# A convolution in float32 or in half-precision halves: the banded product of the later batches, its scales taken beforehand

## The chip, the core and the metric

The kernel runs on one core of a Trainium2 chip. The metric is the device time of one execution in microseconds (us). The core's engines run side by side, each through its own queue of instructions in order: PE (TensorE, matrix products, with its weight loads shown as PEld), DVE (VectorE), ACT (ScalarE), POOL (GpSimd) and SP (SyncE, which here only issues transfers). They wait for each other by semaphores. Transfers between the chip's memory and the on-chip memory are made by 16 DMA engines.

## The reference

Eight batches of 4224 tokens with 192 channels go through a causal convolution of 7 taps (one set of softmaxed taps for each of 8 groups of 24 channels), a two-dimensional Fourier transform of which the real part is added, a layer norm, and a two-layer network with a residual:

```python
w = softmax(weight)                                  # (8 heads, 7 taps)
x_pad = concat([zeros(B, 6, D), x], axis=1)
conv[b, s, h, g] = sum_k w[h, k] * x_pad[b, s + k, h, g]   # 8 heads of 24 channels
mixed = real(fft(fft(conv, axis=1), axis=2))
u = conv + mixed
un = (u - mean(u)) / sqrt(var(u) + 1e-6)
out = u + relu(un @ w_ch1) @ w_ch2                   # 192 -> 768 -> 192
```

## The kernel before

**The front of a batch.** A batch's tokens are cut into 36 windows of 128 rows that overlap, each giving 120 convolved tokens. Six windows make a chunk; a batch has 6 chunks. `load_windows` (L412) brings a chunk of 128 x 1152 float32 numbers into a tile `xt`, of which there are two. `squares` (L425) takes the sum of its squares on ACT; its written result, `sq`, is thrown away, only the running sum is kept. `conv_unit` multiplies the chunk with a banded matrix `band` (128 x 120, one for each head) in float32 on PE (L472), three heads into one piece of the fast accumulating memory, called `pc`; ACT moves `pc` into `xa` (L477), and SP stores `xa` to the scratch `sc` in memory. In the last batch PE takes only 7 heads; the eighth is done on DVE with multiply-adds (`conv_segments`, L542 and L544).

From all six sums `scales` makes a power of two, `s_x`, by which the batch is multiplied before it is cut into two half-precision numbers: the high half (ACT) and the rest (DVE). This is how every other product of the kernel runs: `a*b` as `a_hi*b_hi + a_hi*b_lo + a_lo*b_hi`. `load_x` reads the convolved tokens back in another order into `xs`, `split_x` makes `XH` (ACT, L633) and `XL` (DVE, L637) of them, and three stages of products, `pa` (L659), `pb` (L685) and `pq` (L755), do the Fourier transform.

**The back of a batch.** The transform's result, a residual, and a layer norm give `u`; its halves are turned by a transposing transfer into `kt`. The hidden layer is `ph` (L892), cut into the halves `hh` by ACT (L896) and `hlo` by DVE (L897); the output layer is `po` (L911, L914, L917). There are two buffers for `ph`, so the third `ph` waits until DVE has written the first one's `hlo`.

**The order.** After an opening, the program is a loop over 72 steps, 9 to a batch: 8 with 512 tokens of the network and one short one, the ninth, with 128. In step n of the loop the network of one tile is done, and around its products stand units of the fronts of later batches. `plan` says in which step, counted back from a batch's first network step, which unit stands: for the fourth batch and later the chunks of the convolution at -21 to -16, the scales at -15, the loads of `xs` from -14 and the splits of `xs` from -13. The scheduler that builds the program then sets the order in each engine's queue, down to single products. `in_turn()` puts a unit behind the latest `hh` and `hlo`, and `load_windows` puts its load behind the latest transposing transfer.

## Time and profile before

| what | value |
|---|---|
| runs (3) | 1234.21, 1235.25, 1237.3 us; median 1235.25 |
| profiled execution | 1241.18 us, span 1239.4 us |
| PE busy | 1172.8 us, 95% of the span |
| DVE busy | 807.2 us, 65% |
| ACT busy | 818.6 us, 66% |
| POOL busy | 501.1 us, 40% |
| granted PE clock, mean | 0.985 |
| moved | 170.14 MB, mean 137 GB/s |

The span runs from the first to the last instruction of the profiled execution. "Busy" is the time in which at least one instruction of the engine was under way. Products on PE overlap, so the mean duration of one is longer than the distance between the starts of two. In the rows below, "L472 PE MATMUL pc<-xt,band" reads: line 472, engine PE, operation, written tile, read tiles. A float32 product shows as two passes on PE.

### The profile page before, as it was taken

How to read it: one execution, taken by the hardware profiler on the slowest of the kernel's cores; microseconds unless marked ns; L12 is line 12 of the kernel's file. 1: busy time of each engine (PE TensorE's matmuls, PEld its weight loads, DVE VectorE, ACT ScalarE, POOL GpSimd, SP SyncE). 2: the span in 40 equal slices, each digit the busy share in tenths (PEclk: the TensorE clock that was granted, in tenths of full speed). 3: DMA queues.
4: the chain of work that ended last, by engine and by line, in shares of the span. 5: the costliest groups of instructions: out<-in, count | busy, mean ns of one | idle time of the engine just before them, and what ended most of it. 6: DMA issues, size and time to landing. Idle time of an engine off the chain costs nothing.

```text
span 1239.4 us, 30189 instructions
## 1 busy us (share of the span) xinstructions
PE 1172.8 (95%) x12234; PEld 933.0 (75%) x12234; DVE 807.2 (65%) x1998; ACT 818.6 (66%) x1581; POOL 501.1 (40%) x503
## 2 busy tenths in 40 slices
PE   5278899999999999999999999999999999999999
PEld 4276578787878878787877878788787867777777
DVE  4787575567666666667566676666865786556654
ACT  5476686678657876678656886578665676556542
POOL 2428233355244444445333552444443452346210
PEclk9599999999999999999999999999999999999999
DMA  8856784695435853486535754358452442323321
GB/s 261 316 149 150 163 207 133 171 215 149 108 100 155 211 139 79 120 204 174 136 93 157 190 149 109 96 150 207 108 126 78 122 90 68 78 68 87 74 53 46
DMA packets 225732, 170.14 MB, mean 137 GB/s; under 512 B 119151, under 2 KB 206925, under 8 KB 225592
## 3 DMA queue, kind: packets, MB, share of 16 engines
q1 hardware_dynamic: 212646, 141.03, 45.1%
q0 software_dynamic: 11136, 25.34, 7.0%
q8 instruction: 95, 1.56, 0.5%
q10 hardware_dynamic: 1810, 1.84, 0.5%
q14 instruction: 45, 0.37, 0.1%
HBM read 84.50 MB, written 58.50 MB: 115 GB/s over the span
## 4 chain that ended last, share of the span: by engine, by line
PE 78%; DVE 9%; ACT 5%; DMA 4%; issue 2%; another core or an unknown queue 1%; SPq 1%; POOL 1%; ACTq 0%; DVEq 0%
PE ph L892 30%; PE po L911 9%; PE po L917 9%; PE po L914 9%; PE pa L659 7%; PE pq L755 5%; PE pc L472 5%; PE pb L685 5%; DMA sc<-xa 2%; ACT un L835 1%; DVE XL L637 1%; DVE hlo L897 1%; ACT XH L633 1%; ACT hh L896 1%
## 5 line engine op out<-in xcount | busy, mean ns | idle before, releaser
L892 PE MATMUL ph<-kt,W 128*128 128x512 f16 (+1 forms) x2160 | 494.2, 362 | 9.9 <-DVE hlo L897 7.2
L897 DVE SCALAR_TENSOR_TENSOR hlo<-ph,hh 128x512 f16<-128x512 f32 (+1 forms) x400 | 271.1, 679 | 251.0 <-ACT hh L896 220.2
L896 ACT ACTIVATE hh<-ph 128x512 f16<-128x512 f32 (+1 forms) x400 | 237.2, 594 | 290.3 <-PE ph L892 266.9
L911 PE MATMUL po<-W,hh 128*128 128x192 f16 x1584 | 388.2, 246 | 2.7 <-ACT hh L896 1.7
L914 PE MATMUL po<-W,hh 128*128 128x192 f16 x1584 | 388.1, 246 | 2.2 <-DVE W L394 2.2
L917 PE MATMUL po<-W,hlo 128*128 128x192 f16 x1584 | 388.0, 247 | 1.5 <-DVE hlo L897 1.4
L892 PEld LDWEIGHTS <-W 128*128 128x128 f16 x2160 | 193.5, 98 | 153.1 <-issue 12.6
L791 POOL TENSOR_TENSOR u<-u,xr 128x768 f32<-128x768 f32 (+1 forms) x70 | 119.1, 1702 | 319.6 <-ACT u L790 286.1
L723 POOL DMA_INDIRECT xr<-sc,rows_sb x175 | 193.2, 1104 | 50.5 <-issue 34.8
L849 POOL TENSOR_TENSOR hl<-un,hl 128x512 f16<-128x512 f32 (+1 forms) x144 | 126.1, 898 | 145.9 <-ACT hl L846 120.4
L911 PEld LDWEIGHTS <-hh 128*128 128x128 f16 x1584 | 155.2, 98 | 19.7 <-ACT hh L896 2.2
L917 PEld LDWEIGHTS <-hlo 128*128 128x128 f16 x1584 | 154.9, 98 | 17.8 <-issue 2.6
L914 PEld LDWEIGHTS <-hh 128*128 128x128 f16 x1584 | 155.1, 98 | 16.4 <-issue 0.7
L668 DVE SCALAR_TENSOR_TENSOR yl<-pa,yh 99x512 f16<-99x512 f32 x128 | 86.6, 686 | 66.9 <-ACT yh L667 48.4
L835 ACT ACTIVATE un<-u,nm,y 128x192 f32<-128x192 f32 x256 | 119.5, 544 | 8.0 <-DVE nm L822 5.3
L659 PE MATMUL pa<-c_sb,XH 128*128 128x128 f16 x1024 | 105.5, 222 | 16.7 <-ACT XH L605 16.1
L472 PE MATMUL pc<-xt,band 128*120 128x144 f32 x756 | 109.3, 289 | 4.8 <-DVE V L694 3.4
L472 PEld LDWEIGHTS pc<-xt,band 128*120 128x120 f32 x756 | 100.4, 184 | 13.4 <-DVE V L694 3.8
L659 PEld LDWEIGHTS <-XH 128*128 128x128 f16 x1024 | 84.9, 104 | 28.4 <-ACT XH L605 16.2
L923 DVE SCALAR_TENSOR_TENSOR u<-po,fo,u 128x384 f32<-128x384 f32 (+1 forms) x136 | 80.6, 593 | 37.8 <-PE po L917 29.2
L637 DVE SCALAR_TENSOR_TENSOR XL<-xs,s_x,XH 128x768 f16<-128x768 f32 (+1 forms) x56 | 100.4, 1796 | 6.0 <-ACT XH L633 6.0
L755 PE MATMUL pq<-c_sb,V 128*128 128x130 f16 (+1 forms) x1440 | 96.6, 215 | 2.5 <-issue 2.5
(145 smaller groups left out, 1498.0 us busy)
## 6 DMA issues: line engine op xcount, KB each, us to landing
out_dram<-u SPq DMA_DIRECT2D x64, 384.0 KB
xt<-in_xw_dram SPq DMA_DIRECT2D x36, 576.0 KB
sc<-xa SPq DMA_DIRECT2D x33, 540.0 KB
xs<-sc SPq DMA_DIRECT2D x84, 192.0 KB
xs<-sc SPq DMA_DIRECT2D x28, 216.0 KB
xr<-sc SPq DMA_DIRECT2D x56, 96.0 KB
xt<-in_xv_dram SPq DMA_DIRECT2D x6, 504.0 KB
sc<-xa SPq DMA_DIRECT2D x6, 472.5 KB
```

Of the source, the lines that this page charges most:

```text
L472: nc.tensor.matmul(pc[:WR, h - h0], band[:, h], xt[:, :, h * GRP : (h + 1) * GRP], start=True, stop=True,)
L659: nc.tensor.matmul(pa[:, i], x[:, at], F[:, l], start=(n == 0), stop=(n == 2))
L723: nc.gpsimd.indirect_dma_start(bt.xr[it][:, g], None, bt.sc[: S if b else 128 * LP], bass.IndirectOffsetOnAxis(ap=(rows_sb if b else lines ...
L755: nc.tensor.matmul(po, weights(v, ND * r + k3), rhs[:, 0] if it == Q0 else rhs, start=(r + n == 0), stop=(r == 1 and n == 2),)
L835: nc.scalar.activation(un[:, g], u[:, g], AF.Identity, bias=nm[:, g : g + 1], scale=y[:, g : g + 1],)
L849: nc.gpsimd.tensor_tensor(bl[:, :, o : o + n], un[:, :ng, f], hi[:, :, f], op=ALU.subtract)
L892: nc.tensor.matmul(ph[:, n], W1[:, w, ht * 128 : (ht + 1) * 128], kt[:, k], start=(i == 0), stop=(i == len(order) - 1),)
L896: anchor[0] = nc.scalar.activation(hh, ph, AF.Relu).ins
L897: anchor[1] = nc.vector.scalar_tensor_tensor(hlo, ph, 0.0, hh, op0=ALU.max, op1=ALU.subtract).ins
L911: nc.tensor.matmul(po[:, g % 2], hh[:, ht, tk], W2[:, ht, 0], start=(ht == 0), stop=False)
L914: nc.tensor.matmul(po[:, g % 2], hh[:, ht, tk], W2[:, ht, 1], start=False, stop=False)
L917: nc.tensor.matmul(po[:, g % 2], hlo[:, ht, tk], W2[:, ht, 0], start=False, stop=(ht == 5),)
```

## The change

For batches 5 to 8 of the eight (numbers 4 to 7 in the code):

- Each chunk is loaded twice. The first time only its squares are summed (`measure`); the square is written over the chunk itself. This stands at -26 to -23 (a step later for the first of these batches).
- `scales` moves from -15 to -23 (-22 for the first).
- The second time the chunk is multiplied by the scale and split into halves (`split_window`, ACT and DVE), in the step before its convolution; the halves lie in a fixed tile `CV`.
- `split_band`, once, turns `band` into halves, scaled by 2^14, in place.
- Each head's product is three half-precision products into the same `pc`; ACT multiplies by the inverse scale `cg` as it moves `pc`.
- Loads are no longer issued by the convolution but by whoever has finished with a chunk (`next_load`), in one row over all these batches.
- In the last batch `conv_segments` moves from -16 to -25, and its square comes after its multiply-adds.

The tile `CV` also takes over the places of three smaller ones (the thrown-away squares, the scratch of the weights' conversion, and `w2f`).

```diff
+NB1 = 4
+BSC = 2.0 ** 14
...
+    CV = cp.tile([128, 4, 3 * D], F32, name="CV")
+    sq = CV[:, 0].bitcast(mybir.dt.bfloat16)
...
+    def split_band():
+        f = band.rearrange("p h o -> p (h o)")
+        n = NH * WR
+        hi, lo = (CV[:, i].bitcast(F16)[:, :n] for i in range(2))
+        nc.scalar.activation(hi, f, AF.Copy, scale=BSC)
+        nc.vector.scalar_tensor_tensor(
+            lo, f, BSC, hi, op0=ALU.mult, op1=ALU.subtract
+        )
+        both = f.bitcast(F16)
+        nc.vector.tensor_copy(both[:, :n], hi)
+        nc.vector.tensor_copy(both[:, n:], lo)
...
+    def split_window(bt, ch, l):
+        hi, lo = window_halves(bt, ch)
+        xt = bt.xt[ch]
+        with in_turn():
+            if l == 0:
+                nc.scalar.activation(hi, xt, AF.Copy, scale=bt.c)
+            else:
+                nc.vector.scalar_tensor_tensor(
+                    lo, xt, bt.c, hi, op0=ALU.mult, op1=ALU.subtract
+                )
+                next_load()
...
-            if b > 1:
+            if 1 < b < NB1:
                 squares(bt, xt)
...
+        if b < NB1:
+            terms, scale = ((band, xt),), 1.0
+        else:
+            halves = band.rearrange("p h o -> p (h o)").bitcast(F16).rearrange(
+                "p (l h o) -> p l h o", l=2, h=NH
+            )
+            hi, lo = window_halves(bt, ch)
+            terms, scale = ((halves[:, 0], hi), (halves[:, 0], lo), (halves[:, 1], hi)), bt.cg[:WR]
         for h in range(h0, h0 + n):
-            nc.tensor.matmul(
-                pc[:WR, h - h0], band[:, h], xt[:, :, h * GRP : (h + 1) * GRP],
-                start=True, stop=True,
-            )
-        to = xa[:, :, h0 * GRP : (h0 + n) * GRP].rearrange("p w (h g) -> p h w g", g=GRP)
-        nc.scalar.activation(to, pc[:WR, :n], AF.Copy)
+            for i, (w, x) in enumerate(terms):
+                nc.tensor.matmul(
+                    pc[:WR, h - h0], w[:, h], x[:, :, h * GRP : (h + 1) * GRP],
+                    start=(i == 0), stop=(i == len(terms) - 1),
+                )
+        nc.scalar.activation(to, pc[:WR, :n], AF.Copy, scale=scale)
...
+    def measure(bt, ch):
+        squares(bt, bt.xt[ch], bt.xt[ch])
+        next_load()
+
+    def front_later(bt, rel):
+        units = []
+        first = bt.b == NB1
+        sums_at = (
+            {-25: [0], -24: [1, 2], -23: [3, 4], -22: [5]}
+            if first
+            else {-26: [0], -25: [1, 2], -24: [3, 4], -23: [5]}
+        )
+        if bt.b >= NB0 and rel == -25:
+            units += [call(scratch, bt), call(conv_segments, bt)]
+        if first and rel == -23:
+            units.append(split_band)
+        units += [call(measure, bt, ch) for ch in sums_at.get(rel, ())]
+        if rel == plan(bt.b)[1]:
+            stages = scales(bt)
+            units += [call(next, stages), call(next, stages), call(last, stages)]
+        conv = [call(conv_unit, bt, rel + 21, p) for p in range(3) if -21 <= rel < -15]
+        units += conv
+        if -22 <= rel < -16:
+            if not conv:
+                units += [int] * 4
+            units += [call(split_window, bt, rel + 22, l) for l in range(2)]
+        return units
```

The change moves instructions in three places that matter below.

DVE, in the sixth step of each batch's nine (the rows are those of the fourth batch's): `hlo_5` are the six halves of that step, one for each `ph_5`; `XL` is a split of `xs` for a later batch. Before:

```order
L897 SCALAR_TENSOR_TENSOR hlo_5_9490<-ph_5_1_9532,hh_5_9489 128x512
L694 SCALAR_TENSOR_TENSOR V_0_9540<-pb_0_1_9559,V_0_9540 128x102x4
L923 SCALAR_TENSOR_TENSOR u_4_8480<-po_4_0_9506,fo,u_4_8480 128x384
L897 SCALAR_TENSOR_TENSOR hlo_5_9490<-ph_5_2_9636,hh_5_9489 128x512
L897 SCALAR_TENSOR_TENSOR hlo_5_9490<-ph_5_3_9670,hh_5_9489 128x512
L798 BN_STATS st_8_9682<-u_8_9577 128x6
L637 SCALAR_TENSOR_TENSOR XL<-xs_0_9455,s_x_9195,XH 128x64x12
L923 SCALAR_TENSOR_TENSOR u_4_8480<-po_4_2_9650,fo,u_4_8480 128x384
L799 BN_AGGR mv_8_9683<-st_8_9682 128x2
L897 SCALAR_TENSOR_TENSOR hlo_5_9490<-ph_5_4_9708,hh_5_9489 128x512
L897 SCALAR_TENSOR_TENSOR hlo_5_9490<-ph_5_5_9718,hh_5_9489 128x512
```

With the change:

```order
L939 SCALAR_TENSOR_TENSOR hlo_5_9731<-ph_5_1_9810,hh_5_9730 128x512
L679 SCALAR_TENSOR_TENSOR XL<-xs_0_9649,s_x_7292,XH 128x64x12
L965 SCALAR_TENSOR_TENSOR u_4_8671<-po_4_0_9747,fo,u_4_8671 128x384
L939 SCALAR_TENSOR_TENSOR hlo_5_9731<-ph_5_2_9879,hh_5_9730 128x512
L939 SCALAR_TENSOR_TENSOR hlo_5_9731<-ph_5_3_9912,hh_5_9730 128x512
L840 BN_STATS st_8_9924<-u_8_9819 128x6
L965 SCALAR_TENSOR_TENSOR u_4_8671<-po_4_2_9892,fo,u_4_8671 128x384
L841 BN_AGGR mv_8_9925<-st_8_9924 128x2
L939 SCALAR_TENSOR_TENSOR hlo_5_9731<-ph_5_4_9949,hh_5_9730 128x512
L939 SCALAR_TENSOR_TENSOR hlo_5_9731<-ph_5_5_9960,hh_5_9730 128x512
L474 SCALAR_TENSOR_TENSOR CV<-xt_0_9423,s_x_9722,CV 128x1152
L736 SCALAR_TENSOR_TENSOR V_1_10007<-pb_1_0_10008,V_1_10007 128x102x4
```

The split `XL` went from behind the fourth `hlo_5` to behind the second, and the new split of a chunk, `CV`, stands behind the sixth.

DVE, where the last batch's multiply-adds `sg` stand. Before they begin in the second step of the sixth batch, behind both `XL` of that step:

```order
L897 SCALAR_TENSOR_TENSOR hlo_1_13020<-ph_1_3_13182,hh_1_13019 128x512
L637 SCALAR_TENSOR_TENSOR XL<-xs_3_12651,s_x_11509,XH 128x64x12
L798 BN_STATS st_4_13195<-u_4_13104 128x6 x2
L923 SCALAR_TENSOR_TENSOR u_0_12158<-po_0_2_13162,fo,u_0_12158 128x384
L542 TENSOR_SCALAR sg_13461<-xg_13459,taps 128x792
L799 BN_AGGR mv_4_13196<-st_4_13195 128x2 x2
L897 SCALAR_TENSOR_TENSOR hlo_1_13020<-ph_1_4_13230,hh_1_13019 128x512
```

With the change they begin nine steps earlier, in the second step of the fifth batch, and share it with a chunk's split:

```order
L679 SCALAR_TENSOR_TENSOR XL<-xs_3_10611,s_x_7292,XH 128x64x12
L579 TENSOR_SCALAR sg_11545<-xg_11543,taps 128x792
L581 SCALAR_TENSOR_TENSOR sg_11545<-xg_11543,taps,sg_11545 128x792
L939 SCALAR_TENSOR_TENSOR hlo_1_11016<-ph_1_3_11191,hh_1_11015 128x512
L840 BN_STATS st_4_11214<-u_4_11101 128x6 x2
L581 SCALAR_TENSOR_TENSOR sg_11545<-xg_11543,taps,sg_11545 128x792
L965 SCALAR_TENSOR_TENSOR u_0_10087<-po_0_2_11159,fo,u_0_10087 128x384
L841 BN_AGGR mv_4_11215<-st_4_11214 128x2 x2
L581 SCALAR_TENSOR_TENSOR sg_11545<-xg_11543,taps,sg_11545 128x792
L939 SCALAR_TENSOR_TENSOR hlo_1_11016<-ph_1_4_11251,hh_1_11015 128x512
L474 SCALAR_TENSOR_TENSOR CV<-xt_5_10778,s_x_9722,CV 128x1152
```

Two of the seven now stand between the third and the fourth `hlo_1`, where there was only `XL`, and the chunk's split follows the fifth.

SP, between two transposing transfers `kt` of the fourth batch; `xt` are loads of chunks, `xr` and `out_dram` the network's own. Before:

```order
L859 DMA_TRANSPOSE kt_5_9173<-hl_5_9104 128x12x128
L931 DMA out_dram<-u_2_8049 128x768
L714 DMA xr_1_9801<-sc_5299 128x1x192
L859 DMA_TRANSPOSE kt_6_9468<-hl_6_9410 128x12x128
L931 DMA out_dram<-u_3_8294 128x768
L412 DMA xt_0_9487<-in_xw_dram 128x1152
```

With the change:

```order
L901 DMA_TRANSPOSE kt_5_9405<-hl_5_9351 128x12x128
L973 DMA out_dram<-u_2_8208 128x768
L411 DMA xt_5_9408<-in_xw_dram 128x1152
L411 DMA xt_0_9423<-in_xw_dram 128x1152
L756 DMA xr_1_10044<-sc_5302 128x1x192
L411 DMA xt_1_9690<-in_xw_dram 128x1152
L973 DMA out_dram<-u_3_8468 128x768
L901 DMA_TRANSPOSE kt_6_9704<-hl_6_9654 128x12x128
```

Three loads stand between the two transposing transfers where there was none; each waits for ACT to have squared the chunk that lay in its tile.

More of the change, by code (lines that the diff above doesn't have):

```diff
@@ L338, in square_w @@
             mlp["n" + name] = sb.tile([128, 2], F32, tag="nrm2", name=f"nrm_{name}")
-        sq = sb.tile(
-            [128, 1152], mybir.dt.bfloat16, tag="sq", name=f"sq_{name}_{col}", bufs=1
-        )
         nc.scalar.activation(
@@ L354, in convert @@
         else:
-            bits, aux = (
-                sb.tile([128, 3 * D], F32, tag=f"cv{i}", name=f"cv{i}_{name}", bufs=1)
-                for i in range(2)
-            )
+            bits, aux = CV[:, 1], CV[:, 2]
             if name[-1] == "0":
-                dst = cp.tile([128, 3 * D], F32, name="w2f")
+                dst = CV[:, 3]
             else:
@@ L413, in load_windows, with squares @@
         bt.xt[ch] = xt
-    def squares(bt, x):
+    def squares(bt, x, to=None):
         if bt.nsq == 0:
@@ L418, in squares @@
         n = x.shape[1] if len(x.shape) == 2 else x.shape[1] * x.shape[2]
-        sq = sb.tile(
-            [128, 1152], mybir.dt.bfloat16, tag="sq", name=f"sq_{bt.b}_{bt.nsq}", bufs=1
-        )[:, :n]
-        if len(x.shape) == 3:
-            sq = sq.rearrange("p (w d) -> p w d", w=x.shape[1])
+        if to is None:
+            to = sq[:, :n]
+            if len(x.shape) == 3:
+                to = to.rearrange("p (w d) -> p w d", w=x.shape[1])
         with in_turn():
             nc.scalar.activation(
-                sq, x, AF.Square, accum_out=bt.nrm[:, bt.nsq : bt.nsq + 1]
+                to, x, AF.Square, accum_out=bt.nrm[:, bt.nsq : bt.nsq + 1]
             )
@@ L448, in scratch, with window_halves @@
         bt.sc = dp.tile([S + DUP, D], F32, tag="sc", name=f"sc_{bt.b}", bufs=4)
+    def split_band():
[9 more added lines that the diff above has]
+        nc.vector.tensor_copy(both[:, n:], lo)
+    def window_halves(bt, ch):
+        n = WC * bt.xt[ch].shape[2]
+        return tuple(
+            CV[:, 2 * (ch % 2) + l].bitcast(F16)[:, :n].rearrange("p (w d) -> p w d", w=WC)
+            for l in range(2)
+        )
[10 more added lines that the diff above has]
+                next_load()
     def conv_unit(bt, ch, part, xa_slot=("xa", 2)):
@@ L454, in conv_unit @@
         if part == 0:
-            if ch == 0:
+            if ch == 0 and b < NB0:
                 scratch(bt)
-            if b > 1:
+            if 1 < b < NB1:
                 squares(bt, xt)
@@ L534, in conv_segments @@
         acc = sb.tile([128, SR, DH], F32, tag="xs", name=f"sg_{bt.b}", bufs=2)
-        squares(bt, x.rearrange("p r d -> p (r d)"))
         for i in range(NH - HP):
@@ L546, in conv_segments @@
                     )
+        flat = x.rearrange("p r d -> p (r d)")
+        squares(bt, flat, flat)
         for base, n in ((0, 128), (S, 32)):
@@ L560, in scales @@
         nc.vector.reciprocal(bt.g, bt.c)
+        if bt.b >= NB1:
+            bt.cg = sb.tile([128, 1], F32, tag="cg", name=f"cg_{bt.b}")
+            nc.vector.tensor_scalar_mul(bt.cg, bt.g, 1.0 / BSC)
         nc.vector.tensor_scalar_mul(bt.g, bt.g, GSC)
@@ L981, in plan, with later_loads, next_load @@
         splits = {-13: [0], -12: [1], -11: [2, 3], -10: [4], -9: [5], -8: [6, 7]}
-        return {r: [r + 21] for r in range(-21, -15)}, -15, loads, splits, later_a
+        scales_at = -15 if b < NB1 else -22 if b == NB1 else -23
+        return {r: [r + 21] for r in range(-21, -15)}, scales_at, loads, splits, later_a
+    def later_loads():
+        for b in range(NB1, B):
+            for k in range(2 * NCH):
+                yield b, k % NCH
+    wanted = later_loads()
+    def next_load():
+        b, ch = next(wanted, (None, 0))
+        if b:
+            load_windows(batches[b], ch)
+    def measure(bt, ch):
[8 more added lines that the diff above has]
+            else {-26: [0], -25: [1, 2], -24: [3, 4], -23: [5]}
+        )
+        if bt.b >= NB0 and rel == -25:
[13 more added lines that the diff above has]
+        return units
     def front(bt, rel):
@@ L986, in front @@
         conv, scales_at, load_at, split_at, a_at = plan(bt.b)
-        if bt.b >= NB0 and rel == scales_at - 1:
-            units.append(call(conv_segments, bt))
+        if bt.b >= NB1:
+            units, conv, scales_at = front_later(bt, rel), {}, None
         for ch in conv.get(rel, ()):
@@ L992, in front @@
                 units.append(call(load_windows, bt, ch + 2))
+            if bt.b == NB1 - 1 and ch + 2 >= NCH:
+                units.append(next_load)
         if bt.b == 2 and rel == min(conv) - 1:
             units += [call(load_windows, bt, ch) for ch in range(2)]
-        if bt.b > 2 and rel in (min(conv) - 2, min(conv) - 1):
+        if bt.b > 2 and conv and rel in (min(conv) - 2, min(conv) - 1):
             units.append(call(load_windows, bt, rel - min(conv) + 2))
```

2 lines of the change are left out of this document (1 added, 1 removed).

## The prediction, as it was put on record before the run

> **What bounds the kernel now.** First the page: span, busy times, and the span in 40 slices.
>
> ```profile
> span 1239.4 us, 30189 instructions
> PE 1172.8 (95%) x12234; PEld 933.0 (75%) x12234; DVE 807.2 (65%) x1998; ACT 818.6 (66%) x1581; POOL 501.1 (40%) x503
> ...
> PE   5278899999999999999999999999999999999999
> ...
> PEclk9599999999999999999999999999999999999999
> ```
>
> After the opening, some 200 us, PE is busy in every slice, at nearly the full granted clock. "Busy" does not say that PE runs at its pace, since products overlap; so I go to single steps of the loop. The windows below (bounds: the first `ph` of a step, from the timeline) are the sixth step of the fourth batch, the ninth, and the first three of the fifth batch; the columns are the width, then busy time with counts of PE, PEld, DVE, ACT and POOL, then clock, DMA share and GB/s.
>
> ```profile
> 641.20:657.40 16.20, 15.57 (x178) 11.78 (x177) 9.17 (x20) 9.28 (x17) 6.61 (x7) 1.00 0.39 106
> 690.90:701.20 10.30, 10.30 (x144) 10.30 (x143) 5.93 (x16) 8.87 (x18) 3.75 (x5) 1.00 1.07 246
> 701.20:716.70 15.50, 15.50 (x171) 11.97 (x170) 10.21 (x24) 12.34 (x27) 8.87 (x10) 1.00 0.73 187
> 716.70:732.20 15.50, 15.50 (x141) 11.99 (x139) 12.09 (x31) 14.11 (x26) 9.36 (x9) 1.00 0.56 152
> 732.20:750.10 17.90, 17.90 (x184) 14.54 (x182) 11.36 (x32) 12.00 (x24) 6.50 (x7) 1.00 0.63 155
> ```
>
> PE fills its window in all but the first. Whether it also runs at its pace, the chain of waits tells (start, length, what): it runs for long stretches from product to product on PE itself.
>
> ```profile
> 644.67 1.16 PE pq L755 x35
> 677.89 1.02 PE pq L755 x18
> 699.42 1.98 PE pc L472 x16
> 703.96 2.19 PE pb L685 x48
> 706.15 2.16 PE ph L892 x10
> 843.59 1.74 PE pc L472 x14
> ```
>
> The half-precision products take 2190/48 = 45.6 ns for 102 columns, 1020/18 = 56.7 for 130 and 216 for 512: about 0.416 ns a column and 2.7 ns beside. So PE streams; what is taken from it there is taken from the time. Where it idles in this part, DVE is what it waits for, in two places only:
>
> ```profile
> 657.38 1.24 PE L892 MATMUL ph<-kt,W 128*128 128x512 f16 x5 [0.63 <-DVE hlo L897]
> 876.85 1.24 PE L892 MATMUL ph<-kt,W 128*128 128x512 f16 x5 [0.92 <-DVE hlo L897]
> 893.31 1.24 PE L892 MATMUL ph<-kt,W 128*128 128x512 f16 x5 [0.30 <-DVE hlo L897]
> 896.20 0.26 PE L911 MATMUL po<-W,hh 128*128 128x192 f16 x1 [0.63 <-ACT hh L896]
> ```
>
> **The product on PE.** These are the groups of instructions, the first from a window that holds the convolutions of the last four batches alone.
>
> ```profile
> L472 PE MATMUL pc<-xt,band 128*120 128x144 f32 x372 | 55.1, 288 | 0.0
> L472 PEld LDWEIGHTS pc<-xt,band 128*120 128x120 f32 x756 | 100.4, 184 | 13.4 <-DVE V L694 3.8 <-ACT xa L477 1.4 <-DVE band L234 1.0
> L755 PEld LDWEIGHTS <-V 128*64 128x64 f16 x288 | 9.6, 111 | 3.6 <-issue 3.2
> L892 PEld LDWEIGHTS <-W 128*128 128x128 f16 x2160 | 193.5, 98 | 153.1 <-issue 12.6 <-DMA kt<-hl 1.9
> ```
>
> 372 passes are 186 float32 products (18 chunks of 8 heads, 6 of 7). By the chain 16 passes take 1.98 us and 14 take 1.74: 248 ns for a head. Three half-precision products of 144 columns, between the 56.7 of 130 and the next wider, come to 2.7 + 144 x 0.416 = 62.6 ns each, 188 a head. That is 60 ns less, over 186 heads **-11.2 us**. It lies wholly on PE's path.
>
> This needs the weight loads to stay hidden: one of 120 columns every 62.6 ns, where float32 had one every 124. The trace has no half-precision load of 120 columns. Two rows bound it: float32 loads of 120 columns keep up with 124 ns, at twice the bytes; half-precision loads of 64 columns keep up with 1160/35 = 33 ns, which makes 62 ns for 120. Both ends come to 62, the products' own pace, so I take them as hidden, with a thin margin. The full duration of a load, 111 ns, would be the price if none ran ahead of its product (a rival, below).
>
> The 64-column loads take longer (111 ns) than the 128-column ones (98), so width 128 has a quicker way. The Trainium skill says why ("TensorE: Matmul & The Clock Gate", "Weight-path perf modes"): the fast weight load is on for exactly 128 columns that are not float32, so 120 columns would go without it; and the same page ("LDWEIGHTS") gives columns/1.2 ns, 100 ns for 120. By that figure a head would take 300 ns and the change lose 186 x 52 ns = 9.7 us. The trace disagrees with the figure: 64 columns would then need 53 ns, and they keep up with 33.
>
> **The splits.** Each of 24 chunks gets one more ACT instruction (to the high half) and one more DVE instruction (the rest). Nearest rows are the splits of the weights, contiguous as these are, and the square of the same width:
>
> ```profile
> L379 DVE SCALAR_TENSOR_TENSOR W<-w1a,s_w,W 128x768 f16<-128x768 f32 x1 | 1.0, 1018 | 0.0
> L394 DVE SCALAR_TENSOR_TENSOR W<-w2f,s_w,W 128x576 f16<-128x576 f32 x1 | 0.9, 869 | 0.0
> L371 ACT ACTIVATE W<-w1a,s_w 128x768 f16<-128x768 f32 x1 | 0.9, 922 | 0.0
> L425 ACT ACTIVATE sq<-xt 128x1152 bf16<-128x1152 f32 x42 | 49.1, 1169 | 3.6 <-DMA xt<-in_xw_dram 3.6
> L425 ACT ACTIVATION_READ_ACCUMULATOR sq<-xt 128x1 f32 x48 | 9.9, 206 | 0.0
> ```
>
> DVE: 1018 + 384 x (1018 - 869)/192 = 1316 ns, and 1.5 us if it grows with the width alone; I take 1.4, in all 34 us. ACT: 1.2 us, in all 29. Both are behind PE's work: they stand in the sixth to the ninth and the first two steps of each nine. The tightest is the second (716.70): DVE 12.09 + 1.4 of 15.0 us, ACT 14.11 + 1.2 of the same, so ACT is full. But the convolution's square leaves this step and another's comes last in it, and the third step has 6 us of room. If a DVE split delays PE by half of itself in each tight step (two a batch), the cost is 4 x 2 x 0.7 = 5.6 us; if it hides, 0. I take **+1.0**.
>
> The squares stay as many as they were (1169 + 206 ns); what they write becomes float32 in place, a form the trace lacks. At twice the write time it would add 1.2 us to ACT in steps that have 6 to 7 us free: 0 either way. Splitting `band` is five small instructions in one step, hidden too.
>
> **What moves on DVE.** At 657.38 PE waits for `hlo`, because this stands ahead of it (DVE's timeline, and the waits in total):
>
> ```profile
> 653.80 2.35 DVE L637 SCALAR_TENSOR_TENSOR XL<-xs,s_x,XH 128x768 f16<-128x768 f32 x1
> ```
>
> It recurs once in each of four batches. With the change `XL` stands two `hlo` earlier, where the next `ph` comes only after 36 `pq` products (1.16 us) and 18 `po` (192 columns, by the line above 82.6 ns each, 1.49 us) and finds DVE done. Gain 4 x 0.63 = 2.5 us if nothing takes its place, 0 if the chunk's split behind the sixth `hlo` does. I take **-1.5**.
>
> The last batch's multiply-adds are seven of these:
>
> ```profile
> L544 DVE SCALAR_TENSOR_TENSOR sg<-xg,taps,sg 128x792 f32<-128x792 f32 x6 | 6.2, 1030 | 0.0
> L542 DVE TENSOR_SCALAR sg<-xg,taps 128x792 f32<-128x792 f32 x1 | 1.4, 1440 | 0.0
> ```
>
> 7.6 us. Where they stood PE lost 0.92 + 0.30 + 0.63 = 1.85 us; that goes. Where they go, 716.70 to 750.10, DVE has 12.09 + 11.36 = 23.45 us, and with 7.6 and 1.4 comes to 32.5 of 33.4 - 0.9 = 32.5. PE's `ph` of that step come 2.3 to 3.3 us apart (chain of waits):
>
> ```profile
> 722.08 1.08 PE ph L892 x5
> 724.40 1.08 PE ph L892 x5
> 727.72 1.08 PE ph L892 x5
> ```
>
> From the third `hlo` on the order puts about 4 us of DVE work between two `hlo`; DVE falls about 6 us behind, and the two `ph` buffers cover some 5. I expect 1.2 us of waiting there, at best 0, at worst 5: net **-0.6** (-1.85 to +3).
>
> **Transfers.** 18 x 576 KB + 6 x 504 KB = 13.4 MB more, 3.5 in a stretch of nine steps that moves 144.7 us x 144 GB/s = 21 MB:
>
> ```profile
> 411.90:556.60 144.70, 144.07 (x1532) 115.73 (x1530) 94.33 (x236) 102.25 (x199) 62.67 (x61) 1.00 0.57 144
> ```
>
> The DMA share is 0.39 to 0.73 but for the short ninth step (1.07), where one chunk is loaded as before. A load is issued about a step ahead of its use, 10 to 17 us. On SP three loads now stand ahead of a transposing transfer, and each waits for a square on ACT; behind them wait `xr`, `out` and `kt`, and PE needs `kt` a step later. The squares they wait for stand in the step before, so I cost this at 0; a late load has cost 3 us at worst so far:
>
> ```profile
> POOL u L791 <- DMA xt<-in_xw_dram: 6.1, 2, 3.0
> ```
>
> **Sum.** -11.2 + 1.0 - 1.5 - 0.6 = -12.3 us on the profiled execution's span of 1239.4 us (1241.18 with what lies around it). The runs' median is 1235.25, 0.5% below; the difference is the same there: **1223.0 us**.
>
> **Rivals.**
>
> *The other engines fill up.* ACT at 15.3 of 15.0 us in the second step and DVE at 32.5 of 32.5 where `sg` goes hold `hh` and `hlo` back. For it: these sums. Against: PE lost nothing in that step with ACT at 14.11 of 15.5, and both neighbours have room. At the upper bounds, 5.6 for the splits and 3 for `sg`, with no gain from `XL`: -11.2 + 8.6 = -2.6; about half of that is likelier, -11.2 + 4.3 = -6.9: 1228.
>
> *The weight loads set the pace (slower than before).* Place: each of the 558 new products. If a load does not run ahead, a product takes the load's 111 ns instead of 62.6: 333 a head against 248, 186 x 85 ns = 15.8 us more, 1251. It decides from 83 ns a load on, where the gain is zero. For it: 120 is not 128, and the margin is thin. Against: the 33 ns of the 64-column loads. The skill's 100 ns is this same rival, at 1245.
>
> *The second loads come late.* Four batches with one 3 us wait each on PE eat 12 us: 1235, no change. For it: three loads in a row on SP. Against: they are issued a step ahead.
>
> *More is won*, all of DVE's waits gone and no new ones: -11.2 - 2.5 - 1.85 = -15.6, 1219.7.
>
> **Chances.** Forecast 0.66 (its own range 1219.5 to 1227), engines full 0.18, more 0.04, weight loads 0.06, late loads 0.06. Under 0.3% (3.7 us) a difference cannot be told from none. The first three are faster by more: 0.88, with nearly all of the second in it; same 0.06; slower 0.06. The range 1218.5 to 1232 leaves out the last two and the edges.
>
> **What would show it.** `pc` in the later batches: three products a head, 62 to 63 ns from start to start, 24 in 1.5 us; weight loads in between without gaps. If they are 80 or more apart, the loads set the pace. In the windows of a batch (9 steps) the width falls from 144.7 to about 141.3, by 2.9 for the product and some 0.5 for `XL`. At the sixth step the 0.63 us wait is gone. Where `sg` stands, one or two waits of PE for `hlo`, 1 to 2 us in all. Behind the fifty-first step nothing changes, and nothing ahead of the tenth. The forecast is wrong if PE shows idle time ahead of `pc` with ACT or DVE `CV` as releaser, or behind `kt`.

## The result, and the profile after

| | before | with the change |
|---|---|---|
| median of the runs | 1235.25 us (1231.83 to 1237.3, 15 runs) | 1226.54 us (1224.16 to 1233.09, 15 runs) |
| profiled execution | 1241.18 us, span 1239.4 us | 1226.07 us, span 1224.3 us |

The ratio is 0.9934, 95% interval 0.9921 to 0.9946: 8.7 us, 0.7% faster. Beside the experiments the changed kernel was timed twice more, on the chips called C and D below: 0.9934 (0.9912 to 0.9956) and 0.9967 (0.9953 to 0.9982).

The page of the changed kernel: span and busy times.

```profile
span 1224.3 us, 30643 instructions
PE 1161.2 (95%) x12420; PEld 919.4 (75%) x12420; DVE 848.3 (69%) x2029; ACT 850.9 (70%) x1606; POOL 502.2 (41%) x503
```

PE has lost 11.6 us of busy time, DVE gained 41 and ACT 32. PE's share of the span stays at 95%, and the span is shorter, so most of the new work on DVE and ACT (now 69 and 70%) lies beside PE's. The profiled spans are 15.1 us apart, but 5.6 us of that lie ahead of step 10 and 1.4 behind step 50, where both kernels issue the same instructions in the same order; that is the difference of two executions (a second profile of the kernel before reaches step 10 at 277.1 us, the changed kernel at 277.3). Steps are counted from 0, as in the code. So all that follows is read from the **stretch** from the first `ph` of step 10 to that of step 50, where the change is. Windows of the kernel before, then of the changed one (first the nine steps of the third batch, 18 to 26, that took 144.7 us before, then the whole stretch):

```profile
282.90:932.30 649.40, 644.66 (x6812) 515.85 (x6809) 432.75 (x1068) 455.99 (x884) 277.86 (x265) 1.00 0.56 140
```

```profile
405.50:548.30 142.80, 141.93 (x1577) 112.62 (x1577) 104.19 (x241) 110.07 (x204) 62.56 (x61) 1.00 0.68 169
277.30:918.60 641.30, 636.08 (x7000) 503.66 (x6997) 472.23 (x1099) 488.56 (x909) 278.16 (x265) 1.00 0.67 164
```

8.1 us less in the stretch, close to the 8.7 of the medians. A second profile of the kernel before gave 649.4 again.

The product itself, by the groups of instructions of the stretch, and a piece of PE's timeline (the float32 rows stand in the prediction):

```profile
L511 PE MATMUL pc<-CV,band 128*120 128x144 f16 x558 | 44.8, 226 | 0.0
L511 PEld LDWEIGHTS <-band 128*120 128x120 f16 x558 | 41.6, 133 | 5.4
```

```profile
657.02 0.73 PE L511 MATMUL pc<-CV,band 128*120 128x144 f16 x9
```

No idle time ahead of any of the 558. By the chain of waits nine of them follow one another in 0.56 us, 62.5 ns each. A weight load takes 133 ns from its start to its end and holds nothing up.

PE's waits in the stretch (in all, times, longest), before and after:

```profile
PE ph L892 <- DVE hlo L897: 4.1, 7, 0.9
PE po L911 <- ACT hh L896: 0.6, 1, 0.6
```

```profile
PE ph L934 <- DVE hlo L939: 3.2, 9, 0.6
PE ph L934 <- DMA kt<-hl: 1.1, 2, 0.7
PE po L953 <- ACT hh L938: 0.5, 2, 0.3
```

4.7 us in 8 waits became 4.8 us in 13. The waits did not go away, they moved. Each costs PE about 0.16 us more than the row says, since the idle time counts from the end of the last product, and that runs on behind the point at which the next could have started (five `ph` show as 1.24 us before a gap and take 1.08 in a stream).

To see where, I took from each step's length the time of its products at their own pace (columns x 0.4167 ns + 3 ns; 248 ns for a float32 head). What is left is the **loss** of the step. In us, for the kernel before and for three profiles of the changed one (the second and third from C and D):

| | before | changed | 2nd | 3rd |
|---|---|---|---|---|
| products at their pace | 642.3 | 631.3 | 631.3 | 631.3 |
| sixth steps (14, 23, 32, 41) | 3.8 | 1.3 | 1.3 | 1.3 |
| where `sg` stands (37, 38, 46, 47) | 2.8 | 2.2 | 2.3 | 2.8 |
| second steps (10, 19, 28) | 0.2 | 1.9 | 2.2 | 2.8 |
| eighth steps (16, 25, 34, 43) | -0.2 | 1.2 | 1.2 | 1.2 |
| ninth steps (17, 26, 35, 44) | -0.2 | 1.4 | 3.8 | 0.6 |
| fourth and fifth steps | 1.0 | 1.8 | 1.8 | 1.8 |
| first steps (18, 27, 36, 45) | 0.0 | 0.4 | 2.1 | 3.1 |
| third and seventh steps | -0.4 | -0.3 | -0.3 | -0.3 |
| stretch | 649.4 | 641.3 | 645.7 | 644.6 |

The product gives 11.0 us, the sixth steps 2.6, and on balance some 5.5 us of new losses come back. What those are, the rows show in four places.

*Second steps.* ACT's timeline of the changed kernel at the end of step 28 (start, length), and PE's:

```profile
575.37 0.58 ACT L938 ACTIVATE hh<-ph 128x512 f16<-128x512 f32 x1
575.84 1.25 ACT L472 ACTIVATE CV<-xt,s_x 128x1152 f16<-128x1152 f32 x1
576.99 0.83 ACT L888 ACTIVATE hl<-un 128x768 f16<-128x768 f32 x1
577.72 0.99 ACT L515 ACTIVATE xa<-pc,cg 120x432 f32<-120x432 f32 x2
578.61 1.08 ACT L938 ACTIVATE hh<-ph 128x512 f16<-128x512 f32 x2
...
579.25 0.26 PE L953 MATMUL po<-W,hh 128*128 128x192 f16 x1 [0.25 <-ACT hh L938]
579.98 0.59 PE L934 MATMUL ph<-kt,W 128*128 128x512 f16 x2 [0.33 <-DVE hlo L939]
```

The new split, `hl` and two evictions stand between two `hh`; `hh` comes late, `hlo` after it, and PE waits for both.

*Eighth steps.* DVE's timeline in step 34:

```profile
674.33 3.57 DVE L679 SCALAR_TENSOR_TENSOR XL<-xs,s_x,XH 128x768 f16<-128x768 f32 x2
677.82 0.67 DVE L939 SCALAR_TENSOR_TENSOR hlo<-ph,hh 128x512 f16<-128x512 f32 x1
```

Both `XL` of the step now stand between two `hlo`; before there was an `hlo` between them.

*Ninth steps.* SP's timeline in step 26, before and after (the time is that of issuing):

```profile
547.13 1.96 SPq L859 DMA_TRANSPOSE kt<-hl  x1
549.18 1.90 SPq L438 DMA_DIRECT2D sc<-xa  x2
```

```profile
535.15 1.81 SPq L630 DMA_DIRECT2D xs<-sc  x4
537.07 0.39 SPq L973 DMA_DIRECT2D out_dram<-u  x1
537.56 1.27 SPq L436 DMA_DIRECT2D sc<-xa  x2
538.95 5.83 SPq L901 DMA_TRANSPOSE kt<-hl  x1
```

The stores of a convolved chunk stood behind the transposing transfer and now stand ahead of it, with four loads of `xs` (before, three) and no pause in between (before, 2 us). SP needs 5.8 us to issue that transfer where it took 2.0, and it has, as before, only some 9 us until the next batch's first `ph` needs it. Neither half of this burst does it alone: behind four loads of `xs`, with no such store for 4.5 us, SP took 3.0 us (kernel before, at 896.95), behind two such stores and no load 2.5 us (changed kernel, at 452.74), both without a pause. Nor does the slow issue alone make PE wait: it is there in step 35 too (6.0 us), and PE lost nothing.

*Sixth steps.* Of the 0.63 us waits nothing is left: in DVE's timeline of step 32 `XL` stands between the second and the third `hlo`, and DVE waits for ACT behind it, not PE for DVE. Three of the four steps gain 0.79 us each. The fourth, step 14, gains 0.2: its wait is gone too, but more stops of about 0.1 us each have come, where PE changes between `pq` and `po`.

```profile
638.13 0.68 DVE L939 SCALAR_TENSOR_TENSOR hlo<-ph,hh 128x512 f16<-128x512 f32 x1
638.73 1.66 DVE L679 SCALAR_TENSOR_TENSOR XL<-xs,s_x,XH 128x768 f16<-128x768 f32 x1
641.13 0.69 DVE L939 SCALAR_TENSOR_TENSOR hlo<-ph,hh 128x512 f16<-128x512 f32 x1 [0.23 <-ACT hh L938]
```

### The profile page after: what moved, and what is told of

It is laid out like the page before. It is cut to its first block, busy times and chain, and to the rows that moved or that the text cites. A ratio compares the mean times of both kernels' runs of the same rounds, so it can differ in the third digit from the quotient of the medians.

```text
span 1224.3 us, 30643 instructions
## 1 busy us (share of the span) xinstructions
PE 1161.2 (95%) x12420; PEld 919.4 (75%) x12420; DVE 848.3 (69%) x2029; ACT 850.9 (70%) x1606; POOL 502.2 (41%) x503
## 4 chain that ended last, share of the span: by engine, by line
PE 70%; DVE 12%; ACT 7%; DMA 5%; POOL 3%; issue 2%; SPq 0%; ACTq 0%; DVEq 0%
PE ph L934 27%; PE po L953 8%; PE po L959 8%; PE po L956 8%; PE pa L701 7%; PE pb L727 4%; PE pq L797 4%; PE pc L511 3%; DVE XL L679 2%; DVE hlo L939 2%; ACT XH L675 2%; DMA sc<-xa 2%; POOL xr L765 1%; ACT un L877 1%; DVE y L862 1%
## 5 line engine op out<-in xcount | busy, mean ns | idle before, releaser
L833 POOL TENSOR_TENSOR u<-u,xr 128x768 f32<-128x768 f32 (+1 forms) x70 | 125.9, 1798 | 313.3 <-ACT u L832 313.2
L765 POOL DMA_INDIRECT xr<-sc,rows_sb x175 | 186.1, 1063 | 50.9 <-issue 32.9
L679 DVE SCALAR_TENSOR_TENSOR XL<-xs,s_x,XH 128x768 f16<-128x768 f32 (+1 forms) x56 | 95.7, 1720 | 6.2 <-ACT XH L675 6.2
L701 PE MATMUL pa<-c_sb,XL 128*128 128x128 f16 x512 | 95.4, 220 | 0.2 <-DVE XL L654 0.2
L797 PEld LDWEIGHTS <-V 128*128 128x128 f16 (+1 forms) x1440 | 83.1, 100 | 15.9 <-issue 6.4
```

The lines of the kernel that those rows point to most:

```text
L701: nc.tensor.matmul(pa[:, i], x[:, at], F[:, l], start=(n == 0), stop=(n == 2))
L765: nc.gpsimd.indirect_dma_start(bt.xr[it][:, g], None, bt.sc[: S if b else 128 * LP], bass.IndirectOffsetOnAxis(ap=(rows_sb if b else lines ...
L797: nc.tensor.matmul(po, weights(v, ND * r + k3), rhs[:, 0] if it == Q0 else rhs, start=(r + n == 0), stop=(r == 1 and n == 2),)
L833: nc.gpsimd.tensor_tensor(u[:, :ng], u[:, :ng], xr[:, :ng], op=ALU.add)
```

## The experiments

They ran in three groups of four, each group on one chip: B (the kernel before: 1244.16 us), C (1235.61) and D (1240.79). Ratios are to the kernel before on the same chip. On B and D every kernel of the changed family waits 1.2 to 3.4 us of the stretch ahead of `pb` in the first steps, for nothing that the profile shows; whether the kernel before does so there was not profiled.

**The float32 product in the new schedule (B).** `full` is the place of both halves of a chunk in `CV`, as float32; `band` keeps its float32 numbers.

```diff
-                nc.scalar.activation(hi, xt, AF.Copy, scale=bt.c)
+                nc.scalar.activation(full, xt, AF.Copy, scale=bt.c)
...
-                    lo, xt, bt.c, hi, op0=ALU.mult, op1=ALU.subtract
+                    xt, xt, bt.c, full, op0=ALU.mult, op1=ALU.subtract
...
-            terms, scale = ((halves[:, 0], hi), (halves[:, 0], lo), (halves[:, 1], hi)), bt.cg[:WR]
+            terms, scale = ((band, full),), bt.cg[:WR]
```

> All of the change stays (two loads, early scales, the split instructions on ACT and DVE, the moved work) but the product is float32 again: ACT writes the scaled chunk in float32 into CV, DVE writes the rest over the chunk itself, and one float32 product per head reads CV and the float32 band. Stretch = from the first ph of step 10 to the first ph of step 50 (counted from 0): before 649.4 us, changed 641.3 us. Theory: the product is worth 186 x 60 ns = 11.2 us on PE's path whatever stands beside it, and the rest of the change is a net loss of 3 us: stretch 652.5, time 1226.5 + 11.2 = 1237.7, some 2.5 above the kernel before. By the prediction's own terms for the rest (+1.0 - 1.5 - 0.6 = -1.1) it would be 648.3 and 1234.1, below the kernel before. Rival (ACT and DVE set the pace in these steps, so that PE's gain is mostly slack): under 6 us of difference, stretch 647 or less, time 1232.5 or less.

1247.21 us, ratio 1.0027 (1.0014 to 1.0040): 3 us slower than before. Its stretch, by the windows:

```profile
283.90:937.50 653.60, 648.50 (x6813) 514.81 (x6811) 468.47 (x1099) 487.71 (x909) 272.71 (x265) 1.00 0.65 161
```

So all of the gain is the product's, and the rest of the change is a cost, not the -1.1 of the prediction. How large a cost is less certain than the 3 us suggest: the stretch is 4.2 us longer than that of the kernel before (649.4, on other chips), and 3.5 of these lie in the first steps, where the waits ahead of `pb` stand; all other steps together lose 0.6. Against the changed kernel on D, which shows the same waits ahead of `pb`, the stretch is 9.0 us longer (653.6 to 644.6), not 11: with the longer product the eighth steps lose nothing (-0.2 for 1.2) and the ninth neither (-0.1 for 0.6). There the faster product only brings PE sooner to a wait.

**No splits (B, and again on D beside the changed kernel).**

```diff
+            if bt.b > NB1 or ch > 1:
+                if l == 1:
+                    next_load()
-            if l == 0:
+            elif l == 0:
                 nc.scalar.activation(hi, xt, AF.Copy, scale=bt.c)
```

> The splits of the chunks are left out except for the first two of the fifth batch; the products read what then lies in CV, so the convolution of the last four batches is not computed. Loads, squares, scales, products and evictions stay. Theory: the instructions of the splits on ACT and DVE hold hh and hlo back and cost about 4 us of the stretch: 637.3, time 1222.5. The prediction's term of 1.0 us: 640.3, 1225.5. Rival (the new waits come from the transfers): 641.3, 1226.5, with the waits in the second steps (0.85 us each in steps 19 and 28) unchanged.

B: 1236.8 us, ratio 0.9956 (0.9941 to 0.9972), stretch 643.65, with 3.9 us of waits for nothing visible in it; on its own it does not decide.

> The kernel without the chunks' splits once more, now beside the changed kernel. Theory: without them the waits for hlo in the second steps (19, 28) and the eighth steps go; leaving out the waits for kt and for issue, which vary from run to run, the stretch is 3.5 us shorter than the changed kernel's (in the first run of it: 643.65 less 5.9 of issue less 0.6 of kt = 637.2 against 641.3 less 1.7 = 639.6, which is 2.4, both read from different chips). The prediction's term: 1.0. Rival: nothing but the kt waits separates them, under 0.5.

> The changed kernel as it is, on the same chip as the three beside it. Its stretch was 641.3 and 645.7 us in two executions; the 4.4 us between them are one transposing transfer that landed late at the end of step 44 (PE waited 0.7 and 2.8 us for kt) and what followed it. Expected: 641 to 646 on a chip like those, with PE's wait for kt at the end of step 44 again the part that differs; on a chip like that of the first four experiments 3 to 4 us more, ahead of pb in the steps that begin a batch.

D: 1233.56 us, ratio 0.9938 (0.9924 to 0.9952), against the changed kernel's 1236.84 us and 0.9967: 3.3 us. The stretch of the changed kernel by the windows, and PE's waits in it for `kt` and for nothing visible; then the same of the kernel without splits:

```profile
281.20:925.80 644.60, 637.12 (x6998) 503.81 (x6997) 466.62 (x1099) 486.16 (x909) 278.81 (x265) 1.00 0.66 163
```

```profile
PE pb L727 <- issue: 2.2, 6, 0.5
...
PE ph L934 <- DMA kt<-hl: 0.5, 2, 0.2
```

```profile
281.80:924.80 643.00, 635.91 (x6998) 503.64 (x6995) 434.85 (x1077) 464.71 (x887) 271.46 (x266) 1.00 0.67 163
```

```profile
PE ph L937 <- DMA kt<-hl: 2.8, 3, 2.0
...
PE pb L730 <- issue: 1.8, 6, 0.4
```

Without these waits: 641.9 and 638.4, so the splits cost 3.5 us on this chip, as expected, and not 1.0. They cost it in the second steps (loss 2.8 with them, 0.2 without) and where `sg` stands (2.8, 2.0). In the eighth steps they hardly matter (1.2, 1.0). The first profile loses less in the first two places (1.9 and 2.2); measured from it the splits cost 2.2 us. What stays where `sg` stands without splits is one wait of 1.8 us, behind a multiply-add that took 2.25 us in both runs without splits, in place of 1.0. The changed kernel came out as expected of a chip like B, 3.3 us above its first profile, 2.7 of them in the first steps. A `kt` 2 us late turned up in step 26 of the kernel without splits, so that belongs neither to the splits nor to step 44 alone.

**No second loads (B).**

```diff
-                yield b, k % NCH
+                yield (b if k < NCH else 0), k % NCH
...
+        xt = ones[:, :72].rearrange("p (o d) -> p o d", o=1).to_broadcast([128, n, 72])
```

> The second loads of the chunks are left out (24 transfers, 13.4 MB); the splits, of the same size, read a constant tile in place of the chunk, so the convolution of the last four batches is not computed; nothing else moves in any queue. Theory: PE's waits for kt at the end of the ninth steps (0.41, 0.12 and 0.66 us) and some 0.3 us of other delays go, the rest stays: stretch 640.0, time 1225.2. The prediction's 0 for the transfers: 641.3, 1226.5. Rival (late loads and a crowded memory are what took the missing 3.5 us of the forecast): 638 or less, 1223 or less, with the waits of the second steps gone too.

1239.31 us, ratio 0.9973 (0.9958 to 0.9987); the changed kernel has 0.9967 on D. The transfers fell from 163 to 141 GB/s in the stretch, and the time did not: 645.3 us with 2.3 of waits ahead of `pb` and 0.7 for `kt` leaves 642.3, against 641.9 of the changed kernel on D. The wait for `kt` did not go, against the theory. It stands at the end of step 17, and SP's timeline there shows what is ahead of it:

```profile
399.24 1.80 SPq L634 DMA_DIRECT2D xs<-sc  x4
...
401.63 1.30 SPq L436 DMA_DIRECT2D sc<-xa  x2
403.06 5.81 SPq L905 DMA_TRANSPOSE kt<-hl  x1
```

It is not the second loads: the loads of `xs` and the stores ahead are still there, and so is the slow issue. That moving the stores back behind the transposing transfer would mend it was not tried.

**Squares and multiply-adds later (B).**

```diff
-            else {-26: [0], -25: [1, 2], -24: [3, 4], -23: [5]}
+            else {-25: [0, 1], -24: [2, 3], -23: [4, 5]}
...
-        if bt.b >= NB0 and rel == -25:
+        if bt.b >= NB0 and rel == -24:
```

> In the last three batches the squares of the six chunks stand at -25 to -23, two a step, and no longer one in the second step of a nine (-26); the last batch's multiply-adds stand at -24 in place of -25. Theory: the full second steps lose by one instruction too many, on ACT (a square) and on DVE (the multiply-adds), and the third and fourth steps have room: 0.85 us less in steps 19 and 28, 1.42 + 0.64 in steps 37 and 38 falls to 0.4: stretch 641.3 - 1.1 - 1.7 = 638.5, time 1223.7. Rival (the work only takes its delay along): steps 37 to 39 lose 2 us as before, steps 19 to 21 and 28 to 30 lose 0.8 in another place: 641.3, 1226.5. A third: the scales come too late behind the squares, the first split waits, and it is slower: 644.

1240.47 us, ratio 0.9975 (0.9963 to 0.9988); stretch 645.9. Half of the theory held: steps 19 and 28 lose 0.5 and 0.4 us, where the changed kernel loses 1.3 and 1.2 on D. With the square gone, the order on ACT also put the second split of these steps behind the next `hh`; the run does not tell the two apart. The other half was not tested, for the multiply-adds did not move. They carry no tie to `hlo`, and the scheduler pulled them up into steps 37 and 38 again, where one of them happened to take three times its time and PE waited 2.8 us (DVE's timeline, and the waits):

```profile
729.63 3.00 DVE L581 SCALAR_TENSOR_TENSOR sg<-xg,taps,sg 128x792 f32<-128x792 f32 x1
```

```profile
PE ph L934 <- DVE hlo L939: 4.6, 10, 2.8
```

**Both kernels on one chip (C).** Unchanged, for the comparison.

> The changed kernel as it is, to stand on the same chip as the three beside it. In the four experiments so far, on another chip than the first two profiles, PE waited 3.3 to 5.0 us of the stretch in the steps that begin a batch, ahead of pb and for nothing that the profile shows (issue), which neither of the first two profiles has. Theory: that belongs to the chip and stands in every kernel alike, so this one and the kernel before show it together or not at all, and the difference between them stays 8 us in the stretch (649.4 to 641.3) and 0.7% in the time. Rival: it comes from where the new instructions stand, then only the changed kernels show it.

> The kernel before as it is, profiled on the same chip as the others. Theory: the stretch from step 10 to step 50 is 8 us longer than the changed kernel's on this chip; issue waits ahead of pb, if there are any, within 1 us of the changed kernel's. Rival: none here where the changed kernel has them, and the difference is 5 us or less.

1228.13 us, ratio 0.9934 (0.9912 to 0.9956); the kernel before's stretch is 649.4 here, with the waits it had before and none ahead of `pb`. The changed kernel's is 645.7, 4.4 more than in its first profile, without waits ahead of `pb`. So the difference was 3.7 us in this execution (the slowest of the six of the changed kernel) and not 8, and the reason is neither of the two expected: one late `kt`, in step 44, which the section on the hardware returns to. On this chip the medians still differ by 7.5 us. Why the gain is half as large on D stays open; the waits ahead of `pb` would make up most of it, if the kernel before does not have them there.

**A plain factor in the eviction (C).** In the changed kernel the eviction with a column of factors is slower than the one before without: 617 for 532 ns.

```diff
-            terms, scale = (...), bt.cg[:WR]
+            terms, scale = (...), 2.0 ** -5 / BSC
```

> ACT moves pc with a constant factor (2 to the -19, this data's own) in place of a column of factors in memory. In the changed kernel the eviction of 432 columns takes 617 ns where it took 534 before. Theory: it is the column of factors that costs, so 534 ns here, 72 evictions x 83 ns = 6 us less on ACT; ACT holds PE back in one wait of the second steps alone, so the stretch falls by 1 us or less. Rival 1: ACT is what the splits' delay goes through, 2 to 3 us less. Rival 2: the eviction is slower because of what runs beside it: still about 617 ns.

The group of the changed kernel, then that of the experiment and PE's waits in it:

```profile
L515 ACT ACTIVATE xa<-pc,cg 120x432 f32<-120x432 f32 x48 | 28.7, 617 | 4.3 <-PE pc L511 4.3
```

```profile
L515 ACT ACTIVATE xa<-pc 120x432 f32<-120x432 f32 x52 | 26.4, 526 | 4.1 <-PE pc L511 4.1
```

```profile
PE ph L934 <- DVE hlo L939: 3.3, 9, 1.3
```

So it is the column, about 90 ns each time, 6.5 us of ACT in all. The Trainium skill has it ("ScalarE: Activation LUTs", section "What ACT_TABLE_LOAD costs"): an operand that is a column of 128 numbers adds 93 ns. The trace agrees, and the prediction had left it out. In time it is worth nothing that can be measured: 1227.78 us to 1228.13, ratio 0.9937 (0.9915 to 0.9959), and the second steps lose 1.9 us as in the first profile.

**Weights of 128 columns (D).**

```diff
+            halves = [[
+                band_pad.bitcast(F16)[:, (l * NH + h) * WR :][:, :128] for h in range(NH)
+            ] for l in range(2)]
...
```

> The band's halves are loaded as 128 columns in place of 120 (the eight more belong to the next head, and what they give is not read); the rest is the same. Theory: the loads lie hidden under 62.5 ns products either way: the mean of one falls from 133 ns to 98, as for the other loads of 128 columns, and neither the distance of two products (62.5 ns) nor the stretch moves, but for the kt waits. Rival (the thin margin shows: single loads of 120 columns do hold products back): 558 products by 2 ns or more, 1 us or more less.

The group of its weight loads:

```profile
L513 PEld LDWEIGHTS <-band 128*128 128x128 f16 x558 | 38.5, 98 | 6.4
```

1235.88 us to the changed kernel's 1236.84, ratio 0.9958 (0.9945 to 0.9971) to 0.9967: no difference. The loads became 35 ns shorter and nothing else moved: less the waits for `kt` and ahead of `pb` the stretch is 642.0 us to 641.9. With 120 columns they are hidden; how wide the margin is, this does not show.

**One multiply-add behind each `hlo` (C, and again on D).** The squares as above; `conv_segments` became a row of units, tied to `hlo`.

```diff
+                yield
+                with in_turn():
...
+            bt.sg = conv_segments(bt)
+            units += [call(scratch, bt), call(next, bt.sg)]
+        if bt.b >= NB0 and rel == -24:
+            units += [call(next, bt.sg)] * KS
```

> In the last three batches the squares stand at -25 to -23, two a step. The last batch's multiply-adds stand one behind each hlo from the fourth step on (-24), where before this the scheduler pulled them all into the second step. Theory: what costs in steps 37 and 38 is several long DVE instructions between two hlo, not their sum over a step; one at a time fits behind each hlo, and PE loses 0.4 us there in place of 2.06; the squares give another 1 us, as they did in the last experiment: stretch 2.5 us below the changed kernel's on this chip (638.8 against 641.3). Rival (DVE is full over the batch, the delay goes along): within 1 us of the changed kernel, with 1 us or more of waits for hlo in steps 39 to 41.

> The kernel with the multiply-adds one behind each hlo and the squares two a step, once more beside the changed kernel: its stretch was 638.6 us. Theory: again within 1 us of that, because it also has no transposing transfer behind the loads in step 44; time 4 us below the changed kernel's, which is 0.3%, ratio to the kernel before 0.990. Rival: the first run was a lucky one, with kt in time by chance: within 0.15% of the changed kernel.

C: 1223.05 us against the changed kernel's 1228.13, ratio 0.9904 (0.9882 to 0.9927). D: 1232.78 against 1236.84, ratio 0.9936 (0.9920 to 0.9953). It beats both kernels, the changed one by 0.3 to 0.4% (on C the two intervals overlap, but in 33 of the 36 pairs of runs it is the faster). The distance of 4 us on D came as expected; the ratio of 0.990 and the stretch within 1 us of 638.6 did not, it was 640.9 with 1.7 us of waits ahead of `pb`. The window of the stretch and PE's waits in it, on C:

```profile
277.20:915.80 638.60, 635.65 (x6999) 503.69 (x6997) 473.38 (x1099) 489.44 (x909) 274.50 (x265) 1.00 0.67 165
```

```profile
PE ph L937 <- DVE hlo L942: 2.4, 10, 0.6
PE ph L937 <- DMA kt<-hl: 0.4, 1, 0.4
```

The steps 37, 38, 46 and 47 lose 0.3 us (C) and 0.7 (D) in place of 2.3 and 2.8, the second steps 0.8 and 1.2 in place of 2.2 and 2.8. DVE has as much work as before (473.4 us to 472.2). What counted where `sg` stands was how much of it stood between two `hlo`; the gain in the second steps belongs to the squares and the split, as in the run before. Of the 7.1 us between the stretches on C about half is the late `kt` of the changed kernel's one execution; on D, where neither has much of that, the difference is 3.7 us.

## Why the prediction was right, and where it was not

It forecast 1223.0 us, with 1219.5 to 1227 as its own range; 1226.54 lies at that range's slow end. By its terms, in us of the stretch (first profile):

| step of the prediction | predicted | measured |
|---|---|---|
| product on PE | -11.2 | -11.0 |
| splits | +1.0 | +1.8 in the second steps, 2.2 to 3.5 in all by the run without them |
| `XL` moved | -1.5 | -2.6 in the sixth steps, +1.4 in the eighth |
| `sg` moved | -0.6 | -0.5 |
| transfers | 0 | +1.6 in the ninth steps |
| not foreseen | | +0.8 in the fourth and fifth steps, +0.4 in the first |
| sum | -12.3 | -8.1 |

- **Product: right.** 62.5 ns where 62.6 was worked out, hidden loads, no wait ahead of `pc`. What was too simple is "It lies wholly on PE's path": put back to float32, it cost 9.0 us (B to D), since 2 us of it are given back at waits in the eighth and ninth steps.
- **Weight loads: the rival is dead.** The bound from the 64-column loads held; 98 or 133 ns a load made no difference. Whether the margin is thin, no run shows.
- **Splits: this step failed.** "I take +1.0" out of 0 to 5.6; the runs without them showed 2.2 to 3.5. The prediction compared sums over a step (15.3 of 15.0 us) and let the third step's room pay for it. But PE waits for the next `hh` or `hlo`, and between two of those in step 28 stood 3.1 us of ACT. Its own rule for the bad case, 0.7 us in each tight step, fits steps 19 and 28, which lose 0.9 us more than before; it had counted eight such steps.
- **`XL`: right in the sixth steps.** The 2.6 us there are the upper bound of 2.5 in another way: three waits at 0.79 us, not four at 0.63, and little from step 14. That the eighth step now has two of them between two `hlo` stands in the order and was not read. That the 1.4 us there come from it is argued from the rows; no run took it apart.
- **`sg`: the net is right by luck.** The steps that `sg` left gained 2.7 us (1.85 were forecast), those it went to lost 2.2 (1.2 were forecast; waits of 0.62, 0.54 and 0.55 us), and the two errors cancel. That the place was bad was shown by the spread version.
- **Transfers: right in the number that was looked at, wrong in the place.** The second loads cost nothing (642.3 us without them, 641.9 with). The three loads ahead of a transposing transfer, on which the rival was built, did no harm. What did is in the ninth step, where a transposing transfer now follows a burst of loads of `xs` and stores; that it is the burst is argued from the times of issue, no run took it apart. The ninth steps lost 0.6 to 3.8 us by it, by execution, and in the worst one the first step behind another 1.7. Idle time behind `kt` was one of the prediction's own signs that it is wrong: PE had 1.1 us of it in the first profile.
- **Evictions: left out.** The column of factors adds 6.5 us to ACT, but the run without it shows no gain.
- The nine steps of a batch fell by 1.9 us, not the 3.4 that the prediction wanted to see.
- The 0.8 us in the fourth and fifth steps stand where the tiny product of the scales moved from one to the other; nothing tested it.

The rival *the other engines fill up* (1228) describes what held PE back in the second steps and where `sg` went better than the forecast did, and by its working, half of the bounds, 1228 was nearer to the result than 1223. Its "no gain from `XL`" did not come, and the late `kt` is not in it. So the number came out in its range through the product, with a net of the other terms that was 4 us too good.

## What to carry to other kernels

Room on an engine is not a sum over a stage. Where a product waits for a short instruction on another engine, count what stands between two of those, and put long instructions there one at a time: the same work, spread so (and two squares a step), was worth 0.3 to 0.4% here. When a product gets faster, read again the order on every queue, SP's too: stores that now come sooner can close up with the loads ahead of a transfer that has no time to lose.

## What the hardware showed that was not expected

**PE's clock halves behind a slice of 3.41 us in which PE had little to do.** In the second profile of the changed kernel PE waited for `kt` in step 44. The waiting product, then the windows of the 3.41 us up to it and of the 3.41 us behind (the granted clock is the third number from the end):

```profile
839.12 2.29 PE L934 MATMUL ph<-kt,W 128*128 128x512 f16 x5 [2.76 <-DMA kt<-hl]
```

```profile
835.79:839.20 3.41, 0.65 (x11) 0.50 (x9) 0.28 (x2) 3.41 (x9) 1.85 (x2) 1.00 1.11 170
839.20:842.61 3.41, 3.41 (x14) 1.98 (x15) 2.19 (x10) 2.34 (x6) 2.80 (x3) 0.50 0.71 219
```

Five `ph` take 2.29 us in place of 1.24, and by the distances of the products the wait costs 4.5 us, not 2.8. The 2.8 us wait in the experiment with the squares and multiply-adds later did the same (its window, first below). Behind the 1.97 us wait of the kernel without splits the clock stayed whole (its timeline and window on D):

```profile
734.41:737.82 3.41, 2.93 (x12) 1.50 (x12) 3.41 (x7) 0.60 (x1) 0.00 (x0) 0.50 0.88 196
```

```profile
554.76 1.25 PE L937 MATMUL ph<-kt,W 128*128 128x512 f16 x5 [1.97 <-DMA kt<-hl]
```

```profile
554.80:557.80 3.00, 3.00 (x34) 2.41 (x35) 0.85 (x3) 0.78 (x2) 2.39 (x3) 1.00 1.17 359
```

But the length of the wait does not decide. In the opening of the changed kernel's first profile a wait of 3.05 us left the clock whole and one of 1.69 us was followed by half of it:

```profile
117.88 0.33 PE L956 MATMUL po<-W,hh 128*128 128x192 f16 x2 [3.05 <-DVE W L393]
136.37 1.93 PE L934 MATMUL ph<-kt,W 128*128 128x512 f16 x5 [1.69 <-DMA kt<-hl]
```

```profile
119.73:123.15 3.42, 3.42 (x27) 2.09 (x25) 2.12 (x9) 2.49 (x5) 2.51 (x4) 1.00 1.11 214
136.80:140.22 3.42, 3.42 (x10) 1.36 (x9) 1.01 (x4) 1.89 (x3) 0.00 (x0) 0.50 1.04 317
```

In each of the fourteen traces the granted clock changes only at points that lie a whole number of 3.413 us apart. What goes with a fall is how little PE was busy in the slice between two such points: where it was under 44%, the next slice always had 0.50; from 44 to 61% both occur; and no slice over 61% was followed by a fall from 1.00. The slice up to 839.20 had 19%, that up to 136.80 32%, that up to 119.73 44%; the 1.97 us lay across two slices with 87 and 56%. So what a wait of 2 to 3 us costs depends on where it falls.

The Trainium skill ("TensorE: Matmul & The Clock Gate", "What's actually happening") has the halved clock come behind an idle window of about 3.4 us. The trace agrees on the length, 3.41 us, and differs on idle: PE was busy for up to 61% of the slice ahead.

**PE stops in a place that no engine's row names.** On B and D the 48 products `pb` of a batch's first step stop for up to 1.1 us at a time with "issue" as the releaser, 1.2 to 3.4 us in a stretch; on C and in the first profiles never. On B and D only kernels of the changed family were profiled, so whether it is the chip or the change is open. The products there are short (45.6 ns) and nothing else is late. What they wait for is not in the profile.
